# Attention with a two-matrix MLP on one core: one PSUM tile for all scores, and the second parts of w_out on VectorE

## The chip, the core and the metric

One core of a Trainium2 chip runs the whole kernel. The metric is the device time of one execution in microseconds (us), the median of the runs. The profile adds one execution taken by the hardware profiler, whose span runs from the first to the last instruction.

Five engines work beside each other, each through its own instructions in a fixed order: TensorE (PE, matmuls; PEld is its weight load), VectorE (DVE), ScalarE (ACT), GpSimd (POOL) and SyncE (SP, which issues the DMAs). They wait for each other through semaphores. PSUM, where matmuls put their results, has eight banks of 512 fp32 words per partition.

## The reference

Eight batches of attention with eight heads, 576 positions and head size 64, where each row keeps only the scores within tau of its largest one, and then an MLP with x*sigmoid(x) on all 4608 tokens:

```python
scores = scale * np.matmul(q, k.transpose(0, 1, 3, 2))          # 8 x 8 x 576 x 576
thresh = np.max(scores, axis=-1, keepdims=True) - tau
scores = np.where(scores >= thresh, scores, -1000000000.0)
scores = scores - np.max(scores, axis=-1, keepdims=True)
attn = np.exp(scores)
attn = attn / (np.sum(attn, axis=-1, keepdims=True) + 1e-09)
x = np.matmul(attn, v)              # as 4608 x 512
h = x @ w_in                        # 512 x 2048
g = h * (1.0 / (1.0 + np.exp(-h)))
return g @ w_out                    # 2048 x 512
```

## The kernel before, in words

**Tiles.** A tile is 128 rows of queries against all 576 keys. A head has 4.5 of them, so two heads make nine tiles, of which one joins the last half tiles of both heads; a batch has 36 and the kernel 288. I count them 0 to 287. The names in the program (`s_192`, `sm_192`, `w32_192`) count empty slots too: from batch 1 on, a name's number is the tile's plus 13.

**Steps of a tile.** `scores` (L403 to L427) multiplies queries and keys into PSUM, in two operands `khi` and `klo`, each in two matmuls of 288 columns: four matmuls, and eight for the joined tile. The first 16 tiles (`direct`, L412) use two fp32 matmuls. `soft1` (L429) lets DVE find the row maxima (L434) and a threshold (L437). `soft1b` (L443) is ACT's exp from PSUM into `w32` (L444). `soft2` (L448) is DVE's mask and row sum (L453), which reads the scores in PSUM a second time, and then two small steps (L457, L461). `soft2b` scales the row (ACT, L466). `soft3` splits it into two fp16 parts (ACT L475 or POOL L477, then POOL L480 and L483) and sends it through a transposing DMA (L493). `av` (L498) is 28 matmuls with v (L508).

**MLP.** `h_unit` (L544) is 12 matmuls (L551) with four steps after them, ACT and DVE in turn (L559, L560, L566, L567). `o_unit` (L575) is 12 matmuls (L582) in each quarter, and one ACT step and a store after the fourth. Between two tiles the main loop (L733 to L782) hands out MLP units at a rate.

**Weights.** Both matrices come as int64 words and are turned into fp32 (`decode_weights`, L184) and then into two fp16 parts (`split_weights`, L216): POOL scales in place (L220), ACT rounds to the first part (L223), POOL subtracts for the second (L224). There are 16 pieces of w_in and 16 of w_out, each 128x512. The ones of w_out are split at program slots 22 to 26.

**Places for scores.** The pool `ps_s` (L71) gives each tile's scores two banks, 288 columns in each, and has two such buffers. So the matmuls of tile t+2 wait until L453 of tile t has read the buffer; the two buffers are separate tiles to the scheduler.

**Order.** A scheduler places the instructions of each engine by its own times and by priorities (`PRI_S` 1600 for scores, L42), and puts a wait wherever two instructions touch the same tile and one of them writes. What stands in each engine's order is fixed before the run.

Of the kernel before, what the change touches and what calls it, by code (L numbers as in the profile page):

```python
# [11 lines left out]
F32 = mybir.dt.float32  # L12
F32R = mybir.dt.float32r
I32 = mybir.dt.int32
AF = mybir.ActivationFunctionType
ALU = mybir.AluOpType
AX = mybir.AxisListType
PSUM = bass.MemoryType.PSUM

P = 128  # L20
B, H, S, D = 8, 8, 576, 64
NPAIR = H // 2
DM, DFF = 512, 2048
NK = DM // P
NF = DFF // P
HALF = S // 2
# [26 lines left out]
def attention_moe(  # L53
# [10 lines left out]
    nc = tc.nc  # L64
# [3 lines left out]
    xp = [ctx.enter_context(tc.tile_pool(name="x0", bufs=1))]  # L68
    stage_ctx = ExitStack()
    stage = stage_ctx.enter_context(tc.tile_pool(name="stage", bufs=2))  # L70
    ps_s = ctx.enter_context(tc.tile_pool(name="ps_s", bufs=2, space=PSUM))  # L71
    ps_m = ctx.enter_context(tc.tile_pool(name="ps_m", bufs=1, space=PSUM))
    ps_a = ctx.enter_context(tc.tile_pool(name="ps_a", bufs=1, space=PSUM))

# [3 lines left out]
    def bank(shape, name, own=None):  # L78
# [10 lines left out]
        out=gate, in0=tau_sb, scalar1=0.0, scalar2=0.125, op0=ALU.is_ge, op1=ALU.mult  # L89
# [3 lines left out]
        out=ntau, in0=tau_sb, scalar1=0.0, scalar2=-1.0, op0=ALU.max, op1=ALU.mult  # L93
# [6 lines left out]
    for i in range(2):  # L100
        t = const.tile([P, S + 64], F32R, name=f"qstack{i}")
# [55 lines left out]
    w16 = wst.bitcast(F16)  # L157
# [58 lines left out]
    def split_weights(i):  # L216
        w = wst[:, i + WSPARE, :]
        hi = w16[:, i, 0:512]
        sc = wsc["in" if i < 4 * NK else "out"][:, 0:1]
        nc.gpsimd.tensor_scalar(  # L220
            out=w, in0=w, scalar1=sc, scalar2=1.0, op0=ALU.mult, op1=ALU.mult
        )
        nc.scalar.activation(hi, w, AF.Copy)  # L223
        nc.gpsimd.tensor_tensor(  # L224
            out=w16[:, i, 512:1024], in0=w, in1=hi, op=ALU.subtract
        )
# [80 lines left out]
    def qcol(h, i):  # L307


        return i * P if h % 2 == 0 else (0, 384, 512, 128, 256)[(i + 1) % 5]  # L310
# [33 lines left out]
    for i in range(2):  # L344
        t = gbuf.bitcast(F32)[:, 4096 + 512 * i : 4608 + 512 * i]
# [49 lines left out]


    sps = {}
    wtile = {}
    small = {}
    wT = {}  # L400
    tiles = []

    def scores(t):  # L403
        v, parts = tiles[t]
        s_ps = ps_s.tile([P, 2, 512], F32, tag="s", name=f"s_{t}")
        sps[t] = s_ps
        if v in direct:
            (h, i, _, _) = parts[0]
            qt, kt = direct[v]
            o = (h % 2) * 256 + i * P  # L410
            for j in range(2):
                nc.tensor.matmul(  # L412
                    s_ps[:, j, :HALF], qt[:, o : o + P],
                    kt[:, j * HALF : (j + 1) * HALF], start=True, stop=True,
                )
            return
        seq = [
            (qstack[h % 2][:, qcol(h, i) : qcol(h, i) + P], kk)
            for h, i, _, _ in parts
            for kk in khl[h]  # L420
        ]
        for n, (lhs, kk) in enumerate(seq):
            for j in range(2):
                nc.tensor.matmul(  # L424
                    s_ps[:, j, :HALF], lhs, kk[:, j * HALF : (j + 1) * HALF],
                    start=(n == 0), stop=(n == len(seq) - 1),
                )  # L427

    def soft1(t):  # L429
        s_ps = sps[t]  # L430
        sm = sb.tile([P, 5], F32, tag="small", name=f"sm_{t}", bufs=4)
        w = sb.tile([P, S], F32, tag="w32", name=f"w32_{t}", bufs=4)
        negm = sm[:, 0:1]
        nc.vector.tensor_reduce(  # L434
            out=negm, in_=s_ps[:, :, :HALF], op=ALU.max, axis=AX.XY, negate=True
        )
        nc.vector.tensor_scalar(  # L437
            out=sm[:, 1:2], in0=negm, scalar1=-1.0, scalar2=ntau, op0=ALU.mult, op1=ALU.add
        )
        small[t] = sm  # L440
        wtile[t] = w

    def soft1b(t):  # L443
        nc.scalar.activation(  # L444
            wtile[t].rearrange("p (j c) -> p j c", j=2), sps[t][:, :, :HALF], AF.Exp,
            bias=small[t][:, 0:1],
        )

    def soft2(t):
        s_ps = sps.pop(t)  # L450
        sm, w = small[t], wtile[t]
        w3 = w.rearrange("p (j c) -> p j c", j=2)
        nc.vector.scalar_tensor_tensor(  # L453
            out=w3, in0=s_ps[:, :, :HALF], scalar=sm[:, 1:2], in1=w3,
            op0=ALU.is_ge, op1=ALU.mult, accum_out=sm[:, 2:3],
        )
        nc.vector.tensor_scalar(  # L457
            out=sm[:, 3:4], in0=sm[:, 2:3], scalar1=1e-9, scalar2=2.0**-12,
            op0=ALU.add, op1=ALU.mult,
        )  # L460
        nc.vector.reciprocal(out=sm[:, 4:5], in_=sm[:, 3:4])  # L461
# [162 lines left out]
    visits = [(0, p, kind) for kind in ("low", "high") for p in range(NPAIR)]  # L624
# [7 lines left out]
    start = {}  # L632
    for v, (b, p, kind) in enumerate(visits):
# [19 lines left out]
        if kind == "low":  # L653
            at(u - LOAD, lambda v=v: load_direct(v))
            at(u - 2, lambda v=v: scale_direct(v))
            c0, n = ranges[0]
# [42 lines left out]
    for first, t0, t1, t2, hp in W_PLAN:  # L699
        for i in range(16):  # L700
            ti = t0 + i * (t1 - t0) / 16
            at(math.floor(ti - 2), pri(hp, lambda i=i + first: load_weights(i)))
            at(math.floor(ti), pri(hp, lambda i=i + first: decode_weights(i)))
        at(t1, pri(hp, scale_out if first else scale_in))
        for i in range(16):
            at(t1 + i * (t2 - t1) // 16, pri(hp, lambda i=i + first: split_weights(i)))
# [22 lines left out]
    def live(t):  # L729
        return 0 <= t < NT and tiles[t] is not None  # L730

    scores(0)
    t = 0  # L733
    while t < NT + 8 or units or ready or held:
        while ready and ready[0][0] <= t:
            _, b, c0, n = ready.pop(0)
# [10 lines left out]
        if live(t):  # L747
            pri(PRI_SOFT1, lambda: soft1(t))()
        if live(t + 1):
            pri(PRI_S, lambda: scores(t + 1))()  # L750
        if live(t - 1):
            soft2b(t - 1)
        if live(t):
            pri(PRI_SOFT1, lambda: soft1b(t))()
# [10 lines left out]
        if live(t):  # L765
            pri(PRI_SOFT2, lambda: soft2(t))()
        for v, p, c0, n in avs.pop(t, []):
# [6 lines left out]
            scale = xscale if v in direct else 2.0**-12  # L774
# [52 lines left out]
```

## Time and profile before

| | us |
|---|---|
| median of 3 runs (lowest, highest) | 1242.41 (1241.87, 1245.1) |
| the profiled execution | 1240.96 |
| its span | 1238.8 |
| PE busy | 1142.8 |
| DVE busy | 931.1 |
| ACT busy | 814.8 |
| POOL busy | 748.6 |

How to read the lines that the prediction shows. The page gives busy time per engine and then the span in 40 slices of 31 us with a digit for each (9 is 90% or more busy). The windows view gives, for each stretch A:B, its length and for each engine the busy time with the number of instructions in brackets, then the granted TensorE clock, the DMA share and GB/s. The view by line and shape ends each row with `| busy us, mean ns of one |` and the idle time just before the group. The view of one line gives the shortest, median and longest duration in ns. A timeline row is start, length, engine, line, instruction, and in square brackets the idle time before it and what ended that. The chain of waits is the chain of work that ended last, in order of time.

### The profile page before, as it was taken

The page shows a single profiled execution, that of the slowest core. Times are in us where ns is not written, and L with a number is a line of the kernel's source. Part 1 is how long each engine was busy: PE and PEld are TensorE (multiplying, and loading weights), DVE is VectorE, ACT ScalarE, POOL GpSimd, SP SyncE. Part 2 cuts the span into 40 slices and gives each one's busy share as a digit, 9 for nine tenths or more (in the row PEclk, how much of TensorE's full clock was granted, in tenths as well). Part 3 has the DMA queues.
Part 4 walks back from the last instruction along what each step waited for, and adds up shares of the span by engine and source line. Part 5 has one row for each costly group of instructions (what it writes and reads, how often), then busy time and mean ns, then how long its engine had stood idle before and what let it go on. Part 6 is the DMA issues. An engine that isn't in the chain of part 4 may idle for free.

```text
span 1238.8 us, 26929 instructions
## 1 busy us (share of the span) xinstructions
PE 1142.8 (92%) x9402; PEld 896.8 (72%) x9402; DVE 931.1 (75%) x2603; ACT 814.8 (66%) x1507; POOL 748.6 (60%) x952
## 2 busy tenths in 40 slices
PE   5776766999899999999999999999999999999998
PEld 3544545777678778777777877787777877777777
DVE  7898866797989998989888859887689848333230
ACT  6888656687677867776777747776677847433331
POOL 1088999788678867886788618783688537200000
PEclk9997887999999999999999999999999999999999
DMA  9669556877878877788787648773688446200000
GB/s 303 183 208 207 129 98 131 158 135 151 163 129 151 160 150 146 154 144 162 141 153 148 123 99 146 157 148 88 118 162 154 83 79 112 52 15 15 14 12 24
DMA packets 363479, 158.15 MB, mean 128 GB/s; under 512 B 329552, under 2 KB 338256, under 8 KB 363344
## 3 DMA queue, kind: packets, MB, share of 16 engines
q1 hardware_dynamic: 363344, 156.43, 62.3%
q8 instruction: 74, 1.21, 0.4%
q14 instruction: 61, 0.50, 0.1%
HBM read 66.72 MB, written 9.44 MB: 61 GB/s over the span
## 4 chain that ended last, share of the span: by engine, by line
PE 64%; DVE 13%; DMA 8%; POOL 5%; ACT 5%; issue 3%; SPq 1%; POOLq 0%; ACTq 0%; DVEq 0%
PE h L551 23%; PE o L582 23%; PE s L424 10%; PE a L508 8%; DMA wT<-hl 3%; DVE w L453 3%; DVE sm L434 3%; DMA vraw<-in_vL 2%; DVE qstack L328 2%; POOL hl L480 2%; ACT w L444 2%; DVE v L289 1%; DMA wraw<-in_w_out 1%; POOL hl L477 1%; ACT w L466 1%
## 5 line engine op out<-in xcount | busy, mean ns | idle before, releaser
L551 PE MATMUL h<-x,wst 128*128 128x288 f16 (+2 forms) x3072 | 430.9, 289 | 14.0 <-DVE gbuf L567 12.0
L582 PE MATMUL o<-gbuf,wst 128*128 128x288 f16 (+2 forms) x3072 | 426.2, 288 | 4.9 <-ACT wst L592 2.5
L551 PEld LDWEIGHTS <-wst 128*128 128x128 f16 x3072 | 292.6, 99 | 102.8 <-issue 22.1
L582 PEld LDWEIGHTS <-wst 128*128 128x128 f16 x3072 | 294.5, 99 | 89.5 <-issue 9.1
L480 POOL TENSOR_TENSOR hl<-w,hl 128x512 f16<-128x512 f32 x272 | 325.3, 1196 | 15.7 <-DMA kraw<-in_kT 3.5
L477 POOL TENSOR_SCALAR hl<-w 128x576 f16<-128x576 f32 x264 | 178.8, 680 | 198.4 <-ACT w L466 128.3
L444 ACT ACTIVATE w<-s,sm 128x576 f32<-128x576 f32 x288 | 210.1, 737 | 81.4 <-DVE sm L434 33.8
L453 DVE SCALAR_TENSOR_TENSOR w<-s,sm,w 128x576 f32<-128x576 f32 x288 | 232.5, 812 | 41.4 <-ACT w L444 39.4
L466 ACT ACTIVATE w<-w,sm 128x576 f32<-128x576 f32 x288 | 218.4, 771 | 58.4 <-DVE sm L461 56.5
L434 DVE TENSOR_REDUCE sm<-s 128x1 f32<-128x576 f32 x288 | 215.0, 750 | 42.8 <-PE s L424 41.0
L560 DVE SCALAR_TENSOR_TENSOR h<-th,h 128x288 f32<-128x288 f32 (+2 forms) x256 | 116.5, 456 | 114.5 <-ACT th L559 112.0
L559 ACT ACTIVATE th<-h,msc 128x288 f32<-128x288 f32 (+2 forms) x256 | 126.9, 497 | 105.4 <-PE h L551 103.0
L424 PE MATMUL s<-khi,qstack 128*128 128x288 f32 x608 | 160.6, 346 | 31.3 <-DVE w L453 27.2
L566 ACT ACTIVATE gbuf<-h 128x288 f16<-128x288 f32 (+2 forms) x256 | 103.7, 407 | 81.6 <-DVE h L560 80.5
L567 DVE SCALAR_TENSOR_TENSOR gbuf<-h,gbuf 128x288 f16<-128x288 f32 (+2 forms) x256 | 114.9, 451 | 40.8 <-ACT gbuf L566 39.8
L508 PE MATMUL a<-wT,v 128*64 128x288 f16 (+1 forms) x1680 | 128.7, 295 | 10.2 <-DMA wT<-hl 10.2
L424 PEld LDWEIGHTS s<-khi,qstack 128*128 128x128 f32 x608 | 98.6, 197 | 53.8 <-issue 42.1
L338 POOL TENSOR_TENSOR klo<-kraw,khi 128x576 fp32r<-128x576 f32 x64 | 92.5, 1446 | 71.3 <-ACT khi L336 71.3
L424 PE MATMUL s<-klo,qstack 128*128 128x288 f32 x608 | 133.7, 302 | 0.0
L508 PEld LDWEIGHTS <-v 128*64 128x64 f16 x1680 | 91.3, 111 | 37.0 <-issue 25.0
L424 PEld LDWEIGHTS s<-klo,qstack 128*128 128x128 f32 x608 | 101.5, 196 | 0.5 <-issue 0.2
L483 POOL TENSOR_TENSOR hl<-w,hl 128x64 f16<-128x64 f32 x272 | 101.7, 374 | 0.0
(93 smaller groups left out, 830.6 us busy)
## 6 DMA issues: line engine op xcount, KB each, us to landing
qraw<-in_qT SPq DMA_DIRECT2D x128, 144.0 KB, 3.0
kraw<-in_kT SPq DMA_DIRECT2D x128, 144.0 KB, 3.1
vraw<-in_vL SPq DMA_DIRECT2D x32, 320.0 KB, 3.4
wraw<-in_w_out SPq DMA_DIRECT2D x16, 512.0 KB, 4.4
out_t<-wst SPq DMA_DIRECT2D x56, 144.0 KB, 2.2
wT<-hl SPq DMA_TRANSPOSE x304, 3.4
gbuf<-in_w_in SPq DMA_DIRECT2D x8, 512.0 KB, 7.5
wraw<-in_w_in SPq DMA_DIRECT2D x8, 512.0 KB, 6.0
```

The lines of the kernel that those rows point to most:

```text
L424: nc.tensor.matmul(s_ps[:, j, :HALF], lhs, kk[:, j * HALF : (j + 1) * HALF], start=(n == 0), stop=(n == len(seq) - 1),)
L434: nc.vector.tensor_reduce(out=negm, in_=s_ps[:, :, :HALF], op=ALU.max, axis=AX.XY, negate=True)
L444: nc.scalar.activation(wtile[t].rearrange("p (j c) -> p j c", j=2), sps[t][:, :, :HALF], AF.Exp, bias=small[t][:, 0:1],)
L453: nc.vector.scalar_tensor_tensor(out=w3, in0=s_ps[:, :, :HALF], scalar=sm[:, 1:2], in1=w3, op0=ALU.is_ge, op1=ALU.mult, accum_out=sm[:, 2:3],)
L466: nc.scalar.activation(w, w, AF.Copy, scale=r)
L477: nc.gpsimd.tensor_scalar(out=fl[:, 0:S], in0=w, scalar1=1.0, scalar2=1.0, op0=ALU.mult, op1=ALU.mult)
L480: nc.gpsimd.tensor_tensor(out=fl[:, 640:1152], in0=w[:, 0:512], in1=fl[:, 0:512], op=ALU.subtract)
L508: nc.tensor.matmul(a_ps[odd * D : (odd + 1) * D, :n], vt[:, lo_v, odd, kv, :], wT[v, b * H + 2 * p + odd][:, kw, c0 - base : c0 - base + n ...
L551: nc.tensor.matmul(ph[:, :n], wi(c, f, lo_w), x16[b, lo_x][:, c, c0 : c0 + n], start=(k == 0), stop=(k == 11),)
L559: nc.scalar.activation(th[:, :n], ph[:, :n], AF.Tanh, scale=moe_sc[b][:, 0:1])
L560: nc.vector.scalar_tensor_tensor(out=ph[:, :n], in0=th[:, :n], scalar=1.0, in1=ph[:, :n], op0=ALU.add, op1=ALU.mult,)
L582: nc.tensor.matmul(ps[:, :n], wo(f, d, lo_w), g[:, lo_g, :n], start=(f == 0 and k == 0), stop=(f == NF - 1 and k == 2),)
```

## The change

It has two parts.

**w_out.** For the 16 pieces of w_out, `split_weights` takes no POOL instruction any more. ACT scales while it rounds, and DVE makes the second part in one instruction, (w times scale) minus first part.

**Scores.** The two buffers become one tile `sall` of 2048 words, four banks, which is taken once. `place_scores` gives each tile a stretch of it. In batches 0 and 1 there are three places of 576 columns side by side (0 to 575, 576 to 1151, 1152 to 1727), and since a matmul stays in one bank, its 576 columns are divided at the bank's border: 512 and 64, 448 and 128, 384 and 192. From batch 2 on there are two places, two banks each, with 288 columns in each bank as before.

```diff
-    ps_s = ctx.enter_context(tc.tile_pool(name="ps_s", bufs=2, space=PSUM))
+    ps_s = ctx.enter_context(tc.tile_pool(name="ps_s", bufs=1, space=PSUM))
+    sall = ps_s.tile([P, 2048], F32, name="sall")
...
+        if i >= 4 * NK:
+            nc.scalar.activation(hi, w, AF.Copy, scale=sc)
+            nc.vector.scalar_tensor_tensor(
+                out=w16[:, i, 512:1024], in0=w, scalar=sc, in1=hi, op0=ALU.mult, op1=ALU.subtract
+            )
+            return
...
+    def place_scores(t):
+        n = place[0]
+        place[0] += 1
+        if visits[tiles[t][0]][0] < 2:
+            c = S * (n % 3)
+            own = sall[:, c : c + S]
+            cuts = [c] + [k for k in (512, 1024, 1536) if c < k < c + S] + [c + S]
+            parts = [(sall[:, a:e], a - c, e - c) for a, e in zip(cuts, cuts[1:])]
+        else:
+            own = sall[:, 1024 * (n % 2) : 1024 * (n % 2) + 1024]
+            own = own.rearrange("p (j c) -> p j c", j=2)[:, :, :HALF]
+            parts = [(own[:, j, :], j * HALF, (j + 1) * HALF) for j in range(2)]
+        sps[t] = own
+        return parts
...
-        s_ps = ps_s.tile([P, 2, 512], F32, tag="s", name=f"s_{t}")
-        sps[t] = s_ps
+        own = place_scores(t)
...
-            for j in range(2):
+            for out, c0, c1 in own:
                 nc.tensor.matmul(
-                    s_ps[:, j, :HALF], lhs, kk[:, j * HALF : (j + 1) * HALF],
-                    start=(n == 0), stop=(n == len(seq) - 1),
+                    out, lhs, kk[:, c0:c1], start=(n == 0), stop=(n == len(seq) - 1)
                 )
```

The readers of the scores (L434, L444 and L453 of before; L456, L467 and L475 now) are the same instructions on the new places.

All engines' orders move, because the scheduler sees another tile and other waits. Three places show how. A bracket names the counters that an instruction waits for: `DVE_49` is VectorE's, `PE_49` TensorE's, `Activation_49` ScalarE's, `Pool_49` GpSimd's.

The first is on ACT, where batch 4 ends; `w32_190` from `s_190` or `sall` is the exp of that tile, `w32_190` from itself the row's scaling. Before:

```order
L444 ACTIVATE w32_189_9386<-s_189_9331,sm_189_9385 128x576 [waits DVE_49,Activation_49,Pool_49]
L466 ACTIVATE w32_188_9328<-w32_188_9328,sm_188_9327 128x576 [waits DVE_49]
L526 ACTIVATE x16_4_0_8207<-a_4_2_288_9279 128x288 [waits PE_49]
L444 ACTIVATE w32_190_9439<-s_190_9389,sm_190_9438 128x576 [waits DVE_49,Activation_49,Pool_49]
L559 ACTIVATE th_3_0_10_8579<-h_3_0_10_8538,msc_3_7441 128x288 [waits PE_49]
L466 ACTIVATE w32_189_9386<-w32_189_9386,sm_189_9385 128x576 [waits DVE_49]
```

And now:

```order
L467 ACTIVATE w32_189_9194<-sall_71,sm_189_9193 128x576 [waits PE_49,Activation_49,Pool_49]
L488 ACTIVATE w32_189_9194<-w32_189_9194,sm_189_9193 128x576 [waits DVE_49]
L467 ACTIVATE w32_190_9246<-sall_71,sm_190_9245 128x576 [waits PE_49,Activation_49,Pool_49]
L488 ACTIVATE w32_190_9246<-w32_190_9246,sm_190_9245 128x576 [waits DVE_49]
L343 ACTIVATE khi_41_9471<-kraw_24_41_9369 128x576 [waits DMAHW5_49,PE_49]
L467 ACTIVATE w32_191_9301<-sall_71,sm_191_9300 128x576 [waits PE_49,Activation_49,Pool_49]
```

The exp of a tile waited for DVE (its maxima); now it waits for PE instead. The count that it asks for in the built program is reached by the last score matmul of the next tile. The scaling of tile 189 stood behind the exp of 190, and stands ahead of it now.

The second is on DVE at the same tiles. Before:

```order
L453 SCALAR_TENSOR_TENSOR w32_189_9386,sm_189_9385<-s_189_9331,sm_189_9385,w32_189_9386 128x576 [waits DVE_49,Activation_49]
L434 TENSOR_REDUCE sm_190_9438<-s_190_9389 128x1 [waits PE_49]
L457 TENSOR_SCALAR sm_189_9385<-sm_189_9385 128x1 [waits DVE_49]
L437 TENSOR_SCALAR sm_190_9438<-sm_190_9438,ntau_81 128x1 [waits DVE_49]
L461 RECIPROCAL sm_189_9385<-sm_189_9385 128x1 [waits DVE_49]
```

And now:

```order
L475 SCALAR_TENSOR_TENSOR w32_189_9194,sm_189_9193<-sall_71,sm_189_9193,w32_189_9194 128x576 [waits Activation_49]
L456 TENSOR_REDUCE sm_190_9245<-sall_71 128x1
L479 TENSOR_SCALAR sm_189_9193<-sm_189_9193 128x1 [waits DVE_49]
L460 TENSOR_SCALAR sm_190_9245<-sm_190_9245,ntau_82 128x1 [waits DVE_49]
L483 RECIPROCAL sm_189_9193<-sm_189_9193 128x1 [waits DVE_49]
L475 SCALAR_TENSOR_TENSOR w32_190_9246,sm_190_9245<-sall_71,sm_190_9245,w32_190_9246 128x576 [waits DVE_49,Activation_49]
```

The steps stand as before, but the maxima of a tile wait for nothing: L475 ahead of them waited for the exp, and the exp for the scores of this tile.

The third is on PE, from tile 192 on (`khi_39` are the keys of the last head of batch 4, `khi_40` those of the next batch; `o_` is MLP work, `a_` the product with v). Before:

```order
L582 LDWEIGHTS wst_89
L582 MATMUL o_2_288_2_8462<-gbuf_61,wst_89 128x288
L424 MATMUL s_192_9498<-khi_39_9133,qstack1_87 128x288 [waits DVE_49,PE_49]
L424 MATMUL s_192_9498<-khi_39_9133,qstack1_87 128x288
L424 MATMUL s_192_9498<-klo_39_9135,qstack1_87 128x288 x2
```

And now, where the rows are the scores of tiles 192, 193 and 194 and then the first products with v:

```order
L447 MATMUL sall_71<-khi_39_8944,qstack1_88 128x288 [waits DVE_49]
L447 MATMUL sall_71<-khi_39_8944,qstack1_88 128x288
L447 MATMUL sall_71<-klo_39_8946,qstack1_88 128x288 x2
L447 MATMUL sall_71<-khi_40_9260,qstack0_86 128x288 [waits DVE_49]
L447 MATMUL sall_71<-khi_40_9260,qstack0_86 128x288
L447 MATMUL sall_71<-klo_40_9262,qstack0_86 128x288 [waits Pool_49]
L447 MATMUL sall_71<-klo_40_9262,qstack0_86 128x288
L447 MATMUL sall_71<-khi_40_9260,qstack0_86 128x288 [waits DVE_49]
L447 MATMUL sall_71<-khi_40_9260,qstack0_86 128x288
L447 MATMUL sall_71<-klo_40_9262,qstack0_86 128x288 x2
L530 LDWEIGHTS v16_4_3_9157 [waits DMAHW7_49,DMAHW4_49,DMAHW1_49]
L530 MATMUL a_4_3_0_9550<-wT_23_39_9208,v16_4_3_9157 64x288 [waits PE_49]
```

Tiles follow each other with nothing between them, and the first score matmul waits for DVE: the count is reached by the maxima (L456) of the tile before. Before, it was reached by L453 of the tile two before. This holds for the tiles of all batches, wherever their places lie.

The amounts of PE work between the scores of one tile and the next move too. In batch 4 (tiles 144 to 179) of the changed order, the other matmuls behind each tile's scores number:

0, 28, 34, 1, 29, 16, 15, 15, 15, 15, 15, 43, 39, 33, 16, 15, 29, 48, 36, 52, 52, 40, 49, 52, 16, 39, 36, 33, 44, 46, 39, 34, 19, 0, 0, 0

of which 224 are products with v (L508 of before), 28 in a group. Batches 3 and 5 have the same numbers, and 6 and 7 nearly so; batch 2 has another distribution of the same kind. Behind the scores of the last tile stood 1447 MLP matmuls and 56 products with v; now it is 750 and 56. The totals of all kinds are unchanged.

More of the change, by code (lines that the diff above doesn't have):

```diff
@@ L397, in attention_moe, with like @@
     sps = {}
+    place = [0]
+    def place_scores(t):
[12 more added lines that the diff above has]
+        return parts
+    def like(t, w):
+        return w if len(sps[t].shape) == 2 else w.rearrange("p (j c) -> p j c", j=2)
     wtile = {}
@@ L410, in scores @@
             o = (h % 2) * 256 + i * P
-            for j in range(2):
[L412 to L415, printed above, removed]
+            for out, c0, c1 in own:
+                nc.tensor.matmul(out, qt[:, o : o + P], kt[:, c0:c1], start=True, stop=True)
             return
@@ L422, in scores @@
         for n, (lhs, kk) in enumerate(seq):
-            for j in range(2):
+            for out, c0, c1 in own:
                 nc.tensor.matmul(
-                    s_ps[:, j, :HALF], lhs, kk[:, j * HALF : (j + 1) * HALF],
-                    start=(n == 0), stop=(n == len(seq) - 1),
+                    out, lhs, kk[:, c0:c1], start=(n == 0), stop=(n == len(seq) - 1)
                 )
@@ L434, in soft1 @@
         nc.vector.tensor_reduce(
-            out=negm, in_=s_ps[:, :, :HALF], op=ALU.max, axis=AX.XY, negate=True
+            out=negm, in_=s_ps, op=ALU.max, axis=AX.X if len(s_ps.shape) == 2 else AX.XY,
+            negate=True,
         )
@@ L444, in soft1b @@
         nc.scalar.activation(
-            wtile[t].rearrange("p (j c) -> p j c", j=2), sps[t][:, :, :HALF], AF.Exp,
-            bias=small[t][:, 0:1],
+            like(t, wtile[t]), sps[t], AF.Exp, bias=small[t][:, 0:1]
         )
     def soft2(t):
+        sm = small[t]
+        w3 = like(t, wtile[t])
         s_ps = sps.pop(t)
-        sm, w = small[t], wtile[t]
-        w3 = w.rearrange("p (j c) -> p j c", j=2)
         nc.vector.scalar_tensor_tensor(
-            out=w3, in0=s_ps[:, :, :HALF], scalar=sm[:, 1:2], in1=w3,
+            out=w3, in0=s_ps, scalar=sm[:, 1:2], in1=w3,
             op0=ALU.is_ge, op1=ALU.mult, accum_out=sm[:, 2:3],
```

## The prediction

> **What bounds the kernel now.** I read the page first, for the busy shares and the slices.
>
> ```profile
> span 1238.8 us, 26929 instructions
> PE 1142.8 (92%) x9402; PEld 896.8 (72%) x9402; DVE 931.1 (75%) x2603; ACT 814.8 (66%) x1507; POOL 748.6 (60%) x952
> PE   5776766999899999999999999999999999999998
> ```
>
> PE is at 9 in nearly every slice behind the ninth, so from 300 us on it sets the time. What it lacks lies in front: 96 us of the span in which it does nothing, mostly before 300 us. The windows, cut at these places, give the sizes.
>
> ```profile
> 75.00:177.00 102.00, 68.20 (x480) 51.92 (x478) 78.49 (x211) 76.00 (x143) 97.54 (x109) 0.82 0.74 159
> 177.00:300.00 123.00, 104.33 (x818) 80.12 (x814) 98.39 (x273) 84.51 (x147) 101.51 (x128) 0.93 0.72 138
> 300.00:1055.00 755.00, 736.91 (x6325) 585.73 (x6325) 639.35 (x1822) 537.68 (x982) 531.10 (x690) 1.00 0.72 136
> 1055.00:1239.00 184.00, 180.42 (x1498) 143.62 (x1495) 50.67 (x116) 57.92 (x126) 4.90 (x8) 1.00 0.08 21
> ```
>
> From 75 to 177 us POOL is busy 97.5 of 102 us; from 300 to 1055 PE 737 of 755; behind that only MLP work is left. Where the tiles lie in these stretches I took from the same windows for the row maxima alone (L434, one for each tile).
>
> ```profile
> 0.00:75.00 75.00, 12.60 (x17) 0.95 0.77 242
> 75.00:177.00 102.00, 15.29 (x21) 0.82 0.74 159
> 177.00:300.00 123.00, 26.78 (x36) 0.93 0.72 138
> 300.00:1055.00 755.00, 160.32 (x215) 1.00 0.72 136
> ```
>
> So batch 0 ends at about 177 us (38 maxima by then), batch 1 at about 300, and the other 216 tiles take 755 us: 3.5 us each. In that stretch PE is the bound, not the softmax of single tiles: it has other work while one of them goes through ACT and DVE.
>
> **The change: scores.** It says three tiles in flight instead of two. The orders say otherwise: scores of t+1 wait for the maxima of t, exp of t waits for the scores of t+1, L475 of t for that exp, and the maxima of t+1 stand behind L475 of t. That closes a loop through three engines, once per tile, in all batches. A row gives the length of each link; first the operations, from 297 us on.
>
> ```profile
> L453 DVE SCALAR_TENSOR_TENSOR w<-s,sm,w 128x576 f32<-128x576 f32 x216 | 174.6, 814 | 35.8 <-ACT w L444 34.2
> L466 ACT ACTIVATE w<-w,sm 128x576 f32<-128x576 f32 x216 | 163.8, 771 | 36.0 <-DVE sm L461 34.2 <-DVE v_e L138 1.4
> L434 DVE TENSOR_REDUCE sm<-s 128x1 f32<-128x576 f32 x215 | 160.4, 749 | 16.1 <-PE s L424 14.9
> L444 ACT ACTIVATE w<-s,sm 128x576 f32<-128x576 f32 x214 | 156.4, 738 | 72.7 <-DVE sm L434 27.7 <-DVE sm L457 20.1 <-DVE sm L461 11.3
> ```
>
> The hand-overs between engines, from two places in the timeline where nothing else was in the way:
>
> ```profile
> 167.62 0.82 DVE L453 SCALAR_TENSOR_TENSOR w<-s,sm,w 128x576 f32<-128x576 f32 x1 [1.48 <-ACT w L444]
> 168.59 0.50 PE L424 MATMUL s<-khi,qstack 128*128 128x288 f32 x2 [1.38 <-DVE w L453]
> 168.93 0.42 PE L424 MATMUL s<-klo,qstack 128*128 128x288 f32 x2
> 169.47 0.75 DVE L434 TENSOR_REDUCE sm<-s 128x1 f32<-128x576 f32 x1
> 170.39 0.15 DVE L461 RECIPROCAL sm<-sm 128x1 f32<-128x1 f32 x1
> 170.57 0.78 ACT L466 ACTIVATE w<-w,sm 128x576 f32<-128x576 f32 x1 [0.94 <-DVE sm L461]
> ```
>
> ```profile
> 368.47 0.42 PE L424 MATMUL s<-klo,qstack 128*128 128x288 f32 x2
> 368.93 0.76 DVE L434 TENSOR_REDUCE sm<-s 128x1 f32<-128x576 f32 x1 [0.46 <-PE s L424]
> 369.80 0.74 ACT L444 ACTIVATE w<-s,sm 128x576 f32<-128x576 f32 x1 [0.52 <-DVE sm L434]
> 370.58 0.82 DVE L453 SCALAR_TENSOR_TENSOR w<-s,sm,w 128x576 f32<-128x576 f32 x1 [0.64 <-ACT w L444]
> ```
>
> DVE to PE 0.15 us (167.62 + 0.82 to 168.59); four score matmuls 0.76 from first to last (168.59 to 169.35); PE to DVE 0.04 (368.89 to 368.93), taken for PE to ACT too; ACT to DVE 0.04 (370.54 to 370.58). Between the maxima of tile t and its exp two branches run beside each other: the scores, 0.15 + 0.76 + 0.04 = 0.95; and the small steps, which end 0.32 behind the maxima (170.22 to 170.54), then 0.03 and the scaling 0.771, which now stands ahead of the exp on ACT: 1.12. The loop is 0.749 + 1.12 + 0.738 + 0.04 + 0.814 + 0.03 = 3.49, say **3.5 us**. Without the scaling branch it is 3.3; with other work of ACT or DVE in the way half an operation more, 4.0. A tile goes through in 3.5 us at best, whatever PE could do.
>
> What is queued behind the waits: on PE, behind the waiting score matmul, all MLP matmuls and products with v; on ACT, behind the exp, the scalings and the MLP's steps; on DVE, behind L475, the next maxima. PE loses what a tile's own stretch lacks of 3.5 us, and a full stretch elsewhere gives nothing back. The prices on PE, from the chain of waits:
>
> ```profile
> 231.13 0.53 PE s L424 x4
> 282.43 1.83 PE a L508 x28
> 1211.90 23.53 PE o L582 x192
> ```
>
> Scores 0.53 a tile (twice that for the joined one), a group of products with v 1.83, an MLP matmul 23.53/192 = 0.1226. In batch 4 the counts of the order give 40 x 0.53 + 8 x 1.83 + 764 x 0.1226 = 130 us, which is 3.6 a tile on the mean, and yet 17 of the 36 tiles hold less than 3.5 each and 32.8 together. They will take 17 x 3.5 = 59.5, so 26.7 us of PE are idle. The same count over tiles 72 to 287 gives 780 us of work and 157 idle (138 at 3.3, 208 at 4.0), over batch 1 86 and 56 (51, 69). Before, the same prices give 715 from tile 72 on, where 736.9 were measured: x1.03, so 804 and 89.
>
> **Clock.** Four tiles around each batch's border have nothing but their scores, 0.92 busy in 3.5. The trace has such a gap, with the scores behind it:
>
> ```profile
> 189.74 0.81 PE L424 MATMUL s<-khi,qstack 128*128 128x288 f32 x2 [2.54 <-DVE w L453]
> 190.35 0.68 PE L424 MATMUL s<-klo,qstack 128*128 128x288 f32 x2
> ...
> 193.40 0.42 PE L424 MATMUL s<-klo,qstack 128*128 128x288 f32 x2
> ```
>
> Four matmuls take 1.29 from first to last instead of 0.76 behind 2.54 us without work, and the window 75 to 177 has a granted clock of 0.82. At that speed the score branch is 0.15 + 1.29 + 0.04 = 1.48, 0.36 more than 1.12: four times 1.4 us, and some 3.4 us at half speed when work comes back (from 189.74 until a pair takes 0.42 again, before 193.40), 1.7 more: 3.1 a batch, 22 over seven batches. If the lone tile with one matmul does the same, 36; if nothing drops, 0. I take 22, since the row is the nearest case there is. The Trainium skill, "TensorE: Matmul & The Clock Gate", Part 1, says that the clock halves after an idle window of some 3.4 us; by that rule gaps of 2.6 us would drop nothing and the sum would be 22 lower. The trace disagrees on the size, at 2.54.
>
> **The change: divided matmuls.** In batches 0 and 1 the same four matmuls have 512 and 64 columns and so on; the sum of columns is the same. No row shows 64 columns of this type. From 0 to +0.2 us (a khi and klo matmul each at the price of a 288 one) on 56 tiles: 0 to 11. I take 0: the scaling branch (1.12) covers the score branch (0.95) by 0.17; without that cover it is the 11.
>
> **The change: w_out.** POOL loses 16 scalings and 16 subtractions, DVE gets 16 instructions of 128x512.
>
> ```profile
> L220 POOL TENSOR_SCALAR wst<-wst,o_w_sc x16: 685/688/1376, 142.0 to 154.9; 128x512 f32<-128x512 f32 x16
> L224 POOL TENSOR_TENSOR wst<-wst x32: 1146/1158/1598, 79.8 to 208.7; 128x512 f16<-128x512 f32 x32
> L197 DVE SCALAR_TENSOR_TENSOR wst<-wraw,wst x24: 677/691/1642, 21.5 to 125.7; 128x512 int32<-128x512 int32 x24
> ```
>
> POOL: 16 x (0.688 + 1.158) = 29.5 us less, in the stretch where it is the fullest engine. DVE: by L197, the same form with two inputs, 16 x 0.691 = 11.1 more, up to 16 x 1.642 = 26.3. The long ones are where DVE and POOL meet; the Trainium skill, "SBUF — State Buffer", "Who interferes with whom", has a two-input DVE instruction contend with POOL's reads, and by that the price would lie nearer to 26. ACT's count stays. If POOL alone set this stretch, it would end 29.5 earlier; the loop is late next, 36 x 3.5 = 126 for the batch, under 177. I take 177 for batch 0 as it was: relief and new work together are worth from -27 to +26 (150 to 203), and DVE, a link in the loop twice, gets what POOL gives up.
>
> **The sum.** Behind the last scores stood 1447 + 56 matmuls in 184 us; 750 x 0.1226 + 56 x 1.83/28 = 96 now, and 2 for the last stores: 98. Batch 0 177; batch 1 89 + 56 + 3 = 148; tiles 72 to 287 804 + 157 + 19 = 980; tail 98: span 1403. The profiled execution of before is 1240.96 for 1238.8, +2.2: 1405; the median is 1.45 above that execution: **1407 us**.
>
> **Rivals.**
>
> Full tiles late too (1500): where an L453 or a scaling stands ahead of what PE waits for, a tile with more than 3.5 us of work is late by one such operation. For: ACT's and DVE's idle time in the rows above is mostly for each other already. Against: PE idles only 18 us in 755 now. 115 tiles x 0.81 = 93 more: 1500; a half of it 1454.
>
> Chained only where places share a bank (1267): the two places from batch 2 on lie two banks apart and would run as before. The Trainium skill, "PSUM — Partial Sum Buffer", on bank collisions, asks for guards by bank and quadrant, no more. Then batch 1 alone pays, 148 against 123: 1242 + 25 = 1267. Against: the waits stand in the order for places 0 and 1024 as well.
>
> Faster (1213): the loop is covered and POOL's relief felt in full, 1242 - 29.5 = 1213. Place: 75 to 177 us, where POOL is at 97.5 of 102 and PE at 68. It decides if hand-overs cost PE under 29.5 of the 213 us (157 + 56) counted, a seventh: if PE's queue had work at nearly every wait. Against: 17 of 36 tiles have not.
>
> Nothing (1242): both effects small, or the queues take up all. Against: the same.
>
> **Chances.** Forecast 0.78, full tiles late 0.12, bank-wise 0.04, faster 0.04, nothing 0.02. A measurement of this kernel tells 0.3% from no change. Faster 0.04, same 0.02, slower 0.94. The range: low, 3.3 us, no clock loss, batch 0 at 150: 150 + 140 + 942 + 98 + 3.65 = 1334; high, all of 4.0, 203 and 36 together would be 203 + 158 + 1012 + 98 + 36 + 3.65 = 1511, which needs every term at its end; I stop at 1490, which leaves out the last part of the rival at 1500. **1330 to 1490.**
>
> **What would show it.** Right: PE busy about as before (1143) with some 250 us idle; score matmuls on PE waiting for DVE's maxima (L456), exp (L467) for PE, L475 for ACT, each a few tenths to 2.5 us, in batches 2 to 7 too; bare tiles 3.5 us apart (up to 4); PEclk under 10 at the batches' borders; from tile 72 on some 980 us for 215 maxima; the last maxima about 100 us from the end; no L220 for w_out, POOL under 90% before 177 us. Wrong: PE still at 97% behind 300 us (bank-wise, or nothing); a first batch shorter by 25 us or more with a steady rate (faster); bare tiles over 4.5 us apart, or waits of PE at full tiles (1500).

## The result and the profile after

| | before | after |
|---|---|---|
| median of 4 runs, us (lowest, highest) | 1242.22 (1241.87, 1245.1) | 1513.39 (1509.24, 1516.91) |
| ratio of the times, 95% interval | | 1.2175 (1.214 to 1.2211) |
| span of the profiled execution | 1238.8 | 1511.3 |

The forecast was 1407 us with a range of 1330 to 1490: the sign was right, the loss is 271 us where 165 were forecast, and the time lies 23 us above the range. The page's busy shares and granted clock:

```profile
span 1511.3 us, 26635 instructions
PE 1226.1 (81%) x9402; PEld 942.3 (62%) x9402; DVE 933.4 (62%) x2619; ACT 830.5 (55%) x1507; POOL 719.8 (48%) x920
...
PE   5777878844799847998589958999589967998699
...
PEclk8778989965899959999699978999799989999899
```

Over the span no engine is at its limit any more. PE has holes of one slice at regular distances, and the clock falls in the same slices: these are the batches' borders. The waits of PE, summed over the span (engine and line, what it waited for, us, times, longest):

```profile
PE sall L447 <- DVE sm L479: 88.7, 35, 4.1
PE sall L447 <- DVE sm L456: 68.6, 63, 4.7
PE a L530 <- DMA wT<-hl: 20.8, 12, 9.6
PE o L604 <- ACT gbuf L588: 19.3, 16, 3.8
...
PE o L604 <- ACT wst L614: 12.7, 10, 3.4
```

Score matmuls wait 157 us for VectorE, at the maxima (L456) and, by the name that the profile gives, at the small step right behind them (L479). One turn of the loop can be followed where batch 4 begins, in a timeline of that place:

```profile
730.72 0.76 DVE L456 TENSOR_REDUCE sm<-sall 128x1 f32<-128x576 f32 x1
...
731.53 0.85 PE L447 MATMUL sall<-khi,qstack 128*128 128x288 f32 x2 [3.15 <-DVE sm L479]
...
731.83 0.78 ACT L488 ACTIVATE w<-w,sm 128x576 f32<-128x576 f32 x1 [1.88 <-DVE sm L483]
...
732.18 0.68 PE L447 MATMUL sall<-klo,qstack 128*128 128x288 f32 x2
...
732.98 0.74 ACT L467 ACTIVATE w<-sall,sm 128x576 f32<-128x576 f32 x1 [0.37 <-PE sall L447]
...
733.75 0.82 DVE L475 SCALAR_TENSOR_TENSOR w<-sall,sm,w 128x576 f32<-128x576 f32 x1 [1.96 <-ACT w L467]
...
734.49 0.75 DVE L456 TENSOR_REDUCE sm<-sall 128x1 f32<-128x576 f32 x1
...
735.12 3.57 PE L530 MATMUL a<-wT,v 128*64 128x288 f16 x28 [2.26 <-issue]
```

Maxima, scores, exp (released by PE, not by DVE), L475, maxima: 3.77 us from 730.72 to 734.49, each start right behind the end before it. The four score matmuls last 1.33 (731.53 to 732.86), not 0.76, and the products with v that follow take 3.57 us for 28 instead of 1.83: the clock is at half. Where tiles have some work of their own and the clock is full, the maxima follow each other as here, in tiles with 15 or 16 other matmuls:

```profile
763.48 0.76 DVE L456 TENSOR_REDUCE sm<-sall 128x1 f32<-128x576 f32 x1
...
766.94 0.75 DVE L456 TENSOR_REDUCE sm<-sall 128x1 f32<-128x576 f32 x1
...
770.29 0.76 DVE L456 TENSOR_REDUCE sm<-sall 128x1 f32<-128x576 f32 x1
...
773.49 0.75 DVE L456 TENSOR_REDUCE sm<-sall 128x1 f32<-128x576 f32 x1
```

3.46, 3.35 and 3.20 us apart: the loop of 3.3 to 3.5 us that the forecast worked out, though their PE work is 2.4 us. The windows, cut where as many tiles are done as in the forecast's stretches (38, then 36, then the rest, then the tail), give the account:

```profile
0.00:218.00 218.00, 156.78 (x965) 0.83 0.62 166
218.00:388.00 170.00, 114.81 (x766) 0.77 0.52 103
388.00:1400.00 1012.00, 855.99 (x6871) 0.92 0.52 101
1400.00:1512.00 112.00, 98.49 (x806) 0.94 0.08 19
```

These are PE's rows: length, busy time with instructions, granted clock. Busy and idle against the forecast, us:

| stretch | before | forecast | measured | PE busy, forecast and measured | PE idle, forecast and measured |
|---|---|---|---|---|---|
| first 38 maxima | 177 | 177 | 218 | 121, 157 | 56, 61 |
| next 36 | 123 | 148 | 170 | 92, 115 | 56, 55 |
| the others | 755 | 980 | 1012 | 823, 856 | 157, 156 |
| tail | 184 | 98 | 111 | 96, 98 | 2, 13 |

From the second stretch to the last maxima PE's idle time is what was forecast, to 1 us in each. What is more there is busy time, without more matmuls than were counted: 0.77 of 114.8 is 88, and 0.92 of 856 is 788, near the counted work of 86 and 780. The matmuls took longer.

### The profile page after: what moved, and what is told of

It is laid out like the page before. It is cut to its first block, busy times and chain, and to the rows that moved or that the text cites. A ratio compares the mean times of both kernels' runs of the same rounds, so it can differ in the third digit from the quotient of the medians.

```text
span 1511.3 us, 26635 instructions
## 1 busy us (share of the span) xinstructions
PE 1226.1 (81%) x9402; PEld 942.3 (62%) x9402; DVE 933.4 (62%) x2619; ACT 830.5 (55%) x1507; POOL 719.8 (48%) x920
## 4 chain that ended last, share of the span: by engine, by line
PE 53%; DVE 21%; ACT 11%; DMA 7%; issue 5%; POOL 2%; SPq 0%; ACTq 0%; POOLq 0%; DVEq 0%
PE o L604 19%; PE h L573 17%; PE sall L447 8%; PE a L530 6%; DVE w L475 6%; DVE sm L456 6%; ACT w L467 5%; DMA vraw<-in_vL 3%; DMA wT<-hl 2%; DVE qstack L335 2%; ACT w L488 2%; DVE h L582 1%; DVE v L296 1%; DVE gbuf L589 1%; DMA wraw<-in_w_out 1%
## 5 line engine op out<-in xcount | busy, mean ns | idle before, releaser
L475 DVE SCALAR_TENSOR_TENSOR w<-sall,sm,w 128x576 f32<-128x576 f32 x288 | 235.0, 816 | 259.0 <-ACT w L467 256.7
L573 PEld LDWEIGHTS <-wst 128*128 128x128 f16 x3072 | 297.4, 100 | 113.7 <-issue 28.2
L604 PEld LDWEIGHTS <-wst 128*128 128x128 f16 x3072 | 297.4, 99 | 100.2 <-issue 19.1
L447 PE MATMUL sall<-khi,qstack 128*128 128x288 f32 (+3 forms) x608 | 176.0, 375 | 162.4 <-DVE sm L479 88.7
L467 ACT ACTIVATE w<-sall,sm 128x576 f32<-128x576 f32 x288 | 211.7, 735 | 106.9 <-PE sall L447 71.4
L447 PEld LDWEIGHTS sall<-khi,qstack 128*128 128x128 f32 x608 | 106.3, 215 | 224.7 <-DVE sm L479 100.0
L456 DVE TENSOR_REDUCE sm<-sall 128x1 f32<-128x576 f32 x288 | 216.9, 753 | 1.4 <-PE sall L438 0.8
L447 PE MATMUL sall<-klo,qstack 128*128 128x288 f32 (+3 forms) x608 | 149.0, 331 | 0.0
L530 PEld LDWEIGHTS <-v 128*64 128x64 f16 x1680 | 103.1, 120 | 59.6 <-issue 43.3
L345 POOL TENSOR_TENSOR klo<-kraw,khi 128x576 fp32r<-128x576 f32 x64 | 93.4, 1460 | 90.1 <-ACT khi L343 89.9
L447 PEld LDWEIGHTS sall<-klo,qstack 128*128 128x128 f32 x608 | 111.2, 217 | 1.6
L505 POOL TENSOR_TENSOR hl<-w,hl 128x64 f16<-128x64 f32 x272 | 94.8, 348 | 0.0
```

The costliest lines, as they stand in the source:

```text
L447: nc.tensor.matmul(out, lhs, kk[:, c0:c1], start=(n == 0), stop=(n == len(seq) - 1))
L456: nc.vector.tensor_reduce(out=negm, in_=s_ps, op=ALU.max, axis=AX.X if len(s_ps.shape) == 2 else AX.XY, negate=True,)
L467: nc.scalar.activation(like(t, wtile[t]), sps[t], AF.Exp, bias=small[t][:, 0:1])
L475: nc.vector.scalar_tensor_tensor(out=w3, in0=s_ps, scalar=sm[:, 1:2], in1=w3, op0=ALU.is_ge, op1=ALU.mult, accum_out=sm[:, 2:3],)
L530: nc.tensor.matmul(a_ps[odd * D : (odd + 1) * D, :n], vt[:, lo_v, odd, kv, :], wT[v, b * H + 2 * p + odd][:, kw, c0 - base : c0 - base + n ...
L573: nc.tensor.matmul(ph[:, :n], wi(c, f, lo_w), x16[b, lo_x][:, c, c0 : c0 + n], start=(k == 0), stop=(k == 11),)
```

## The experiments

**The parts of the change, each alone.** e1 takes the lines of the w_out part over into the kernel before. e2 has one tile and nothing else of the change:

```diff
+    sall = ps_s.tile([P, 2048], F32, name="sall")
...
+        own = sall[:, 1024 * (n % 2) : 1024 * (n % 2) + 1024]
+        own = own.rearrange("p (j c) -> p j c", j=2)[:, :, :HALF]
```

e3 and e4 have two separate tiles and divide the matmuls of batches 0 and 1 within each; e4 has the w_out part too:

```diff
+        s_ps = ps_s.tile([P, 1024], F32, tag="s", name=f"s_{t}")
+        if visits[tiles[t][0]][0] < 2:
+            c = (0, 64, 128)[n % 3]
+            parts = [(s_ps[:, c:512], 0, 512 - c), (s_ps[:, 512 : c + S], 512 - c, S)]
...
```

> The kernel before with the w_out part of the change alone. Theory T (the loss of 271 us comes from the hand-over through one PSUM tile): no loss here, between 1215 (all of POOL's 29.5 us are felt) and 1248, since DVE's 16 instructions of about 0.7 us lie beside other work. Rival W (the w_out part is what makes batch 0 34 us longer than forecast): 1255 to 1275, with the first batch's last maxima later than 177 us.

> The kernel before with one PSUM tile for both places, which lie two banks apart with 288 columns in each bank as before, in all batches; no division, no third place, w_out as before. Theory T: nearly all of the loss, 1480 to 1520, with score matmuls waiting for the row maxima of the tile before, although the two places share no bank. Rival B (only places that share a bank are chained): about 1242. Rival D (divided matmuls): about 1242 too; the divided ones are in the third kernel.

> The kernel before with its two separate tiles, where in batches 0 and 1 the score matmuls are divided as in the change (512 and 64, 448 and 128, 384 and 192 columns). Theory T: 1240 to 1250 (the same columns; up to 0.2 us in each of the tiles that are not on PE's full stretch). Rival D (narrow f32r matmuls, on PE longer than their columns say, make the granted clock's and batch 0's excess): 1260 to 1280.

> The whole change but for the one tile: two separate PSUM tiles in turn, divided matmuls in batches 0 and 1, w_out's second parts by VectorE. Two tiles in flight in place of the three that the change meant. Theory T: 1215 to 1250, the sum of the first and the third kernel's differences. A rival in which the parts only lose together (a fuller DVE and narrower matmuls): over 1270.

| kernel | us | ratio to before, 95% interval |
|---|---|---|
| e1, w_out alone | 1231.55 | 0.9919 (0.9902 to 0.9936) |
| e2, one tile alone | 1503.0 | one run |
| e3, division alone | 1256.63 | 1.0109 (1.008 to 1.0139) |
| e4, all but the one tile | 1229.44 | 0.9903 (0.988 to 0.9925) |

The one tile is the whole loss. e2 has the places of the kernel before, two banks apart, with the same matmuls, and it has the waits of the changed kernel (scores for the small step L467 behind the maxima, and for the maxima L444):

```profile
PE sall L435 <- DVE sm L467: 95.4, 38, 4.1
PE sall L435 <- DVE sm L444: 62.8, 58, 3.7
```

So the rival by which only places that share a bank are chained is out. With the one tile taken out (e4) the rest of the change is faster than before by 1.0%; it and e1 (0.8%) beat both kernels, by little, but by more than their intervals are wide. The gain of w_out's part lies where the prediction saw POOL as the fullest engine. The windows of e1 for 75 to 177 us (PE, PEld, DVE, ACT, POOL):

```profile
75.00:177.00 102.00, 67.23 (x454) 51.26 (x454) 93.40 (x231) 83.12 (x157) 84.64 (x87) 0.80 0.75 170
```

POOL 84.6 instead of 97.5, VectorE 93.4 instead of 78.5. Of the 29.5 us that POOL loses 10.7 are felt, and VectorE is the fullest engine now.

e3 is slower by 14 us, between the ranges of theory T and rival D, and e4, which divides the same matmuls, isn't. To see whether that is the price of a divided matmul, e12 divides them in all batches, with `< 8` in place of `< 2`:

> The kernel before with the score matmuls divided in all batches, not only in batches 0 and 1 (which cost 14 us alone and nothing beside the w_out part). By the trace a group of four takes 0.84 us from first to last where two halves take 0.76: 0.08 us more, and in batches 2 to 7, where PE is the bound, 240 such groups are 19 us. If the 14 us are the price of the division in batches 0 and 1: 1270 to 1282. If they are the order's: 1255 to 1268.

It took 1254.0 us, 1.0113 (1.009 to 1.0136): no more than e3, with four times as many divided tiles. In full clock a divided group takes 0.84 us from first to last where the halves take 0.76, as in e3's timeline:

```profile
209.11 0.50 PE L439 MATMUL s<-khi,qstack 128*128 128x512 f32 x2 [0.37 <-DVE w L467]
209.45 0.50 PE L439 MATMUL s<-klo,qstack 128*128 128x512 f32 x2
```

At that price the 240 groups of batches 2 to 7 would be 19 us. The windows of the score matmuls alone (PE, PEld) from the first maxima of batch 2 to the last ones, first of before and then of e12, show a part of it:

```profile
294.60:1054.30 759.70, 181.57 (x956) 136.89 (x956) 1.00 0.72 137
```

```profile
292.50:1060.80 768.30, 195.05 (x956) 144.46 (x956) 1.00 0.71 135
```

They are busy 13.5 us longer in e12, 0.06 a group, in a stretch that is 8.6 us longer. So a divided group has a price where PE is the bound, and that e12 takes no longer than e3 looks like an accident: e3's loss lies elsewhere. By the traces e3 is 2 us behind the kernel before when batch 2 begins, though all its divided matmuls lie ahead of that; from there to the last maxima PE idles 27 us instead of 18, and behind them stand 54 more matmuls. That is another order of the same work; why the scheduler makes it, and why it goes away beside the w_out part, is open.

**w_out and the three places within one tile.** e9 is e2 once more, with four executions; e10 adds the w_out part to it; e11 is the changed kernel with w_out as before.

> The one tile alone (two places, no division, w_out as before) once more, timed in rounds, as the base for the next two: about 1503.

> One tile with two places as before, and the w_out part. Theory L (with one tile, ScalarE and VectorE are links of the loop, so w_out's 16 instructions on VectorE lengthen batch 0 where they shortened it with two tiles): 1505 to 1515, batch 0 longer than with the one tile alone (202 us). Rival P (w_out gives its 10.7 us here too, and the three places take 20): 1488 to 1497.

> The changed kernel with w_out as before: one tile, three places and divided matmuls in batches 0 and 1. Theory L: 1500 to 1508, batch 0 at about 202 to 204 us: three places give nothing, since the loop is closed whatever the place, and the division costs less than 0.1 us a tile (the scaling branch covers it). Rival P: 1518 to 1528.

Measured: e9 1509.18 us, 1.215 (1.2098 to 1.2203); e10 1505.0, 1.2129 (1.2101 to 1.2156); e11 1517.06, 1.2231 (1.2199 to 1.2264). The intervals of e9 and e10 overlap: with one tile the w_out part neither costs the 10 us of theory L nor shows the 10.7 of e1. (1505.0 is the lower end of theory L's range, but its base came out at 1509 and not at 1503.) In the traces the first 36 tiles do take longer with it, 202 us instead of 196, but the time doesn't show it. The three places bring nothing: e11 is 0.5% slower than e9 by the medians, the intervals just overlap, and 1517 lies between theory L and rival P. Executions with one tile spread by up to 14 us, those of before by 4 to 7, so less can't be told here. Whether three places gain something where they aren't one tile, no run shows.

**The loop's length.** e7 adds half an exp for each tile to the changed kernel, e8 to the kernel before. These are the lines of e8; in e7 they name the scores' place as it lies there:

```diff
     def soft1b(t):
+        dump = sb.tile([P, HALF], F32, tag="dump", name=f"dump_{t}", bufs=1)
+        nc.scalar.activation(dump, sps[t][:, 0, :HALF], AF.Exp, bias=small[t][:, 0:1])
```

> The changed kernel with one more exp of 288 columns for each tile on ScalarE, into a buffer that nothing reads, ahead of the real one: the loop gets some 0.4 us longer. Theory T (each tile with less than the loop's length of PE work takes the loop's length): by the count of PE work in this kernel's order, the lack of 3.9 us sums to 330 us where that of 3.5 was 253 in the changed kernel: 77 us more, 1570 to 1620 with some of the clock. A rival by which the loop binds nowhere (the loss is PE's order or clock): under 1530, since ACT is busy for 55% of the span only.

> The same exp of 288 columns more for each tile on the kernel before, which has no such loop: theory T expects 1242 to 1262 (ScalarE 66% busy, 118 us more; PE is the bound), far less than the 77 us of the changed kernel.

e7 took 1578.33 us, 65 more than the changed kernel; e8 1255.47, 13 more than before (one execution each). ScalarE's busy time grew by 109 and 106 us (118 had been worked out), and cost five times as much where ScalarE is a link of the loop, although it is less busy there (60% of the span; 73% in e8). The loop binds, and the count of tiles that lack its length gives the size roughly (77 us forecast, 65 measured).

**The clock.** e5 and e6 give PE something to do in the bare tiles, with zero weights and a result that nothing reads:

```diff
...
+        ps = ps_a.tile([P, 512], F32, tag="a", name=f"warm_{t}")
+        for _ in range(10):
+            nc.tensor.matmul(
+                ps[:, :HALF], warm_in, hlt[t - 2][:, :HALF], start=True, stop=True
+            )
```

> The changed kernel with 500 idle matmuls more (ten of 288 columns with zero weights behind the scores of the first tiles of each batch and of most of batch 1's second half), which use the fp16 parts of the tile two before and write to a bank that nothing reads there. The order moves a little: by the count of work in each tile, PE's lack of 3.5 us sums to 245 us instead of 253, so 8 us are expected from that alone. Theory C (what the forecast missed, in the main, is the slow TensorE clock behind gaps of 2.4 to 2.6 us, about 80 us of PE time, which lie on the path): the bare tiles stay at full clock, and the time falls by 40 to 70 us, to 1440 to 1470, though 61 us of matmuls are added. Rival H (the slow matmuls lie in waits that the loop makes anyway): 1495 to 1520. Rival Q (the queue of PE gets only longer): over 1530.

> As the run with 500 idle matmuls, with 620 (the last three tiles of each batch too) and another order: the lack of 3.5 us sums to 235 us. Theory C: 1425 to 1460, with the granted clock over 0.95. Rival H: 1485 to 1510.

e5 took 1485.2 us, 1.1948 (1.192 to 1.1976); e6 1475.85. More matmuls, less time: 28 and 38 us (e6 by one execution). Both lie between theory C and its rival. The pages of e5 and then of e6, and the rows of the idle matmuls in each, show where it comes from:

```profile
PE 1270.2 (86%) x9902; PEld 970.2 (65%) x9902; DVE 931.2 (63%) x2620; ACT 829.9 (56%) x1507; POOL 718.0 (48%) x920
```

```profile
PE 1271.1 (86%) x10022; PEld 973.5 (66%) x10022; DVE 924.1 (63%) x2620; ACT 829.2 (56%) x1507; POOL 713.6 (48%) x920
```

```profile
L419 PE MATMUL warm<-hl,warm_in 128*128 128x288 f16 x500 | 86.0, 330 | 37.2 <-POOL hl L517 36.6 <-DVE x L568 0.4
```

```profile
L419 PE MATMUL warm<-hl,warm_in 128*128 128x288 f16 x620 | 96.5, 308 | 33.1 <-POOL hl L517 32.4 <-DVE x L568 0.4
```

The idle matmuls are busy 86.0 and 96.5 us, where 0.1226 each would be 61 and 76, and they waited 37 and 33 us, nearly all of it for POOL's part of the row. Without them the kernel's own matmuls are busy 1192 and 1185 us, where they took 1226: 34 and 41 us of slow time went.

Beside the 8 and 18 us that the count of work expected, 20 and 20 us were gained. So slow matmuls do lie on the path, but less was gained than went, and how much the rest of them costs was not shown by an experiment.

**Are the MLP's steps in the way?** e13 leaves the four steps behind each `h_unit` out in batches 2 to 7 of the changed kernel, e14 in the kernel before.

> The changed kernel without the four steps behind each h unit in batches 2 to 7 (tanh and the products on ScalarE and VectorE are left out; the matmuls of the second matrix take what lies in the buffer). The count of PE work moves, but its lack of 3.5 us over all tiles sums to 253 us as in the changed kernel. Theory M (the 40 us that batches 2 to 7 took beyond the forecast are PE's waits for these steps, which stand behind the waiting exp on ScalarE, and the slow matmuls behind such waits): 1445 to 1475. Rival (the loop's own length and its slow clock alone): 1495 to 1515.

> The kernel before without the same steps, as the base: PE waits 12 us for them in the whole span, most of it in the first 300 us, so 1228 to 1243.

e13 took 1529.62 us, 16 more than the changed kernel, e14 1233.73, 4 less than before (one execution each, so the 16 are little above the spread). Theory M falls, and its rival's range (up to 1515) is passed too. Behind batch 1 PE's waits for these steps fall from 26.5 to 2.3 us, and the largest waits in the whole of e13 are now:

```profile
PE sall L447 <- DVE sm L479: 140.0, 54, 4.3
PE sall L447 <- DVE sm L456: 52.1, 27, 3.9
PE a L530 <- DMA wT<-hl: 33.5, 21, 9.4
```

PE's order has 240 of the MLP matmuls earlier, ahead of the last scores and not behind them, and yet 47 tiles behind batch 1 with at most one matmul beside their scores, where there were 31. PE idles 180 us from the first maxima of batch 2 to the last maxima, where it idled 158. The counted lack is the same in both orders (253 us over all tiles), so the count doesn't give these 22 us; what does is open.

## Why the prediction was wrong

The mechanism was right, and two of its terms were too small: batch 0, taken at 177 us, took 218, and the slow clock, taken at 22 us, added 78 to PE's busy time from batch 1 on. Without the 41 us of the first the time would have been 1472, and without the 54 us by which the two stretches behind batch 0 ran over it would have been 1459, both inside the range. With every term at its upper end the sum was 1511; these two went past theirs (203 and 36). By the prediction's own steps:

- **What bounds the kernel before**: right as far as tested: in e8 106 us more of ScalarE's time cost 13.
- **The loop, in all batches, wherever the places lie**: right, shown by e2, e4 and e7. Its length was right: 3.20 to 3.46 us in the rows above, and 3.77, 3.86, 4.47 and 3.77 in the four bare tiles at half clock from 718.62 to 734.49, where 3.49 + 0.36 was worked out.
- **157 and 56 us of idle PE**: right to 1 us in the windows, but by luck. A third of it behind batch 1 isn't waiting for maxima, though, but for MLP steps, stores and transposed rows; slow matmuls fill a part of the loop's gaps. The two errors cancelled. (For batch 4 the list gives 769 MLP matmuls and not 764, which leaves the 130 us as they are.)
- **The clock, "22 over seven batches"**: the right mechanism, mis-sized, and the main failure from batch 1 on. Against the counted work the matmuls took 26 us longer in batch 1 and 52 behind it, 78 in all, beyond the upper end of 36. I had counted four bare tiles and one recovery a batch. In batch 1 13 of the last 18 tiles are bare, not four; and behind it the half clock also lasts through waits that aren't for maxima, as in the products with v above (2.26 us of wait, then 28 matmuls in 3.57 us; the scores ahead of them were slow already). How much of the 78 is felt in the time is shown for a part only (e5, e6).
- **"I take 177 for batch 0 as it was"**: failed, 218. It was argued that 36 x 3.5 = 126 lies under 177. But a loop of 3.5 us is one with nothing else in its engines' queues, and in batch 0 ScalarE and VectorE decode and split weights between its links; no turn of it there is under 3.8 us. This is a turn of the changed kernel there:

```profile
128.48 0.75 DVE L456 TENSOR_REDUCE sm<-sall 128x1 f32<-128x576 f32 x1
...
129.27 0.83 DVE L223 SCALAR_TENSOR_TENSOR wst<-wst,o_w_sc 128x512 f16<-128x512 f32 x1
...
130.54 1.13 DVE L223 SCALAR_TENSOR_TENSOR wst<-wst,o_w_sc 128x512 f16<-128x512 f32 x1
...
131.92 0.74 DVE L223 SCALAR_TENSOR_TENSOR wst<-wst,o_w_sc 128x512 f16<-128x512 f32 x1
...
132.58 0.81 DVE L475 SCALAR_TENSOR_TENSOR w<-sall,sm,w 128x576 f32<-128x576 f32 x1
...
133.32 0.74 DVE L456 TENSOR_REDUCE sm<-sall 128x1 f32<-128x576 f32 x1
```

  4.84 us, with three instructions of w_out between two maxima. The windows of this place and of the end of batch 0 (PE, PEld, DVE, ACT, POOL) show which engine is full:

```profile
128.00:157.00 29.00, 17.65 (x120) 13.18 (x118) 29.00 (x61) 27.68 (x53) 16.70 (x17) 0.86 0.49 106
170.00:207.00 37.00, 35.85 (x316) 30.29 (x312) 21.10 (x59) 20.12 (x35) 21.77 (x29) 1.00 0.66 137
```

  First VectorE, busy in all 29 us, and later PE. It isn't w_out's part that makes the 41 us (e10 against e9): without it, in e9, POOL is the full engine there (44.2 of 45 us from 122 to 167). In all kernels with one tile, with and without it, the first 36 tiles lie 193 to 204 us after the first maxima (209 in e7), in those with two tiles 157 to 162. So the one tile makes it. Some of it is work: 965 matmuls stand in this stretch where there were 770. What the loop, the weights and this work each add was not taken apart by a run. The forecast's account didn't close here: 86 us of matmuls left the tail, 65 came up behind batch 1, and I put the rest nowhere.
- **The tail, 98**: 111. I took the last stores' 2 us over, and missed that nothing stands between the last scores and the products with v: PE waits 9.56 us, 7.4 of them in this stretch, until the last row has gone through softmax, split and transposing DMA.

```profile
1407.41 0.93 PE L530 MATMUL a<-wT,v 128*64 128x288 f16 x6 [9.56 <-DMA wT<-hl]
```

- **w_out**: between the ends that were given. The row of the 16 instructions in the changed kernel, by line and shape:

```profile
L223 DVE SCALAR_TENSOR_TENSOR wst<-wst,o_w_sc 128x512 f16<-128x512 f32 x16 | 16.4, 1027 | 0.0
```

  16.4 us, between 11.1 by the median of L197 and 26.3 by its longest. The four that have no POOL instruction beside them took 0.74 us each, and each of the eight above 0.8 us has a POOL instruction with two inputs beside it for 0.5 to 1.9 us. That agrees with the rule of the Trainium skill's "SBUF — State Buffer", "Who interferes with whom" (a VectorE instruction with two inputs in SBUF contends with POOL's reads), without showing it to be the cause. With two tiles the part gains 10.7 us of POOL's 29.5 (e1); with one tile no gain could be told (e10).
- **The divided matmuls**: 0.06 us a group in e12's rows, inside the 0 to 0.2 us. That the loop covers them in the changed kernel was not shown: e11 against e9, which has the three places too, can't tell so little.
- **The rival at 1500** (tiles with more than 3.5 us of work late too) is near the measured time, but not by its mechanism: from the maxima of tile 72 on, the 115 such tiles took 622 us where their work counts 586 (604 with the x1.03 of the prediction), 0.16 to 0.31 us each and not 0.81.

The errors of the four stretches, 41 + 22 + 32 + 13, all have one sign: each cost was taken as if nothing else met it, by my reading.

## What to carry to other kernels

Before two buffers are joined into one tile for the sake of their places, look at what the scheduler makes of it: in the changed order each first score matmul waited for a reader of another place. A loop through three engines costs PE its length in every tile whose own work is shorter, so count the work tile by tile in the order, not its mean. Then close the account of moved instructions over all stretches, and price the matmuls behind each gap by rows at the clock that such a gap leaves.

## What the runs showed of the hardware that was not expected

At the end of batch 1 nearly bare tiles follow each other, and the granted clock (the first number behind the brackets) is at half for 34 us on end:

```profile
354.00:388.00 34.00, 15.27 (x63) 11.83 (x64) 17.04 (x53) 14.35 (x21) 20.41 (x26) 0.50 0.56 114
```

This is a piece of PE's timeline there:

```profile
364.12 0.85 PE L447 MATMUL sall<-khi,qstack 128*128 128x512 f32 x2 [2.44 <-DVE sm L479]
364.78 0.83 PE L447 MATMUL sall<-klo,qstack 128*128 128x512 f32 x2
368.05 0.85 PE L447 MATMUL sall<-khi,qstack 128*128 128x448 f32 x2 [2.44 <-DVE sm L479]
```

Gaps of 2.44 us between groups of 1.5 us are enough to keep it there: four divided matmuls take 1.49 us from first to last here and 0.84 at full clock. Where batch 3 ends, one gap is enough for the drop:

```profile
716.43 0.42 PE L447 MATMUL sall<-klo,qstack 128*128 128x288 f32 x2
719.43 0.85 PE L447 MATMUL sall<-khi,qstack 128*128 128x288 f32 x2 [2.57 <-DVE sm L479]
720.08 0.68 PE L447 MATMUL sall<-klo,qstack 128*128 128x288 f32 x2
```

Ahead of 2.57 us without work a pair takes 0.42 us, behind them 0.68. The Trainium skill, "TensorE: Matmul & The Clock Gate", Part 1, gives an idle window of some 3.4 us for the drop; by that such a gap would leave the clock alone, and the measurement decides. With 500 matmuls more in such gaps the changed kernel was faster by 28 us of 1513 (e5), of which the changed order accounts for 8 by the count.
